# A retention and mixture-of-experts kernel: an attention row's place goes earlier to a weight unit, and work on tables, row ends and decays is moved between queues

## The chip, the core and the metric

The kernel runs on one core of a Trainium2 chip. The metric is the device time of one execution in microseconds (us). Engines are named as in the profile: PE (matrix products), DVE, ACT and POOL (element-wise work), SP (issues DMAs). Each of them takes its instructions in the order in which the program lists them.

## What is computed

Three stages, each feeding the next (reference, cut):

```python
# 1. retention: batch 4, heads 8, sequence 576, head_dim 64
scores = scale * q @ k.T
ret = scores * where(i >= j, gamma[h] ** (i - j), 0)
x = (ret @ v) reshaped to 2304 tokens x 512
# 2. dense layer, d_ff 2048
h = x @ w_in
x = (h * sigmoid(1.702 * h)) @ w_out
# 3. eight experts (d_ff 1024), each token to its best one by cosine similarity
out[mask] = gate_w[mask, None] * (relu(x[mask] @ w1[e]) @ w2[e])
```

## The kernel before, in words

**Attention** (the generator `attention_`) works on 16 "rows" `bp` = batch x pair of heads, 1 MB each from `att` (transposed k and q, then natural k and v), plus the last 64 positions of each sequence ("ends") from `tails` and decay tables `tb` from `tab`. The first 512 positions are four chunks of 128. Rows go in groups, numbered `k` here: group 0 is row 0, group 1 rows 1 and 2, group 2 rows 3 and 4, and so on, group 7 rows 13 and 14, group 8 row 15. For each group PE does: `carried` (state times q, L344), `ends_out` and `scores_end` (L352, L354, L303), `scores` of the next group's first row (L297), `values` (the chunks of this group, L361, between the running states of the next group's rows, L335), then `scores` of the next group's second row. One set of two score banks in PSUM (`sc0`, `sc1`) serves every row, so the next `scores` cannot start before the `masks` of the row before have read them.

- **DVE** does `masks` (L313, two halves), the small products of the ends (L306, L377) and `keep` (L386 or L382: the group's output out of PSUM).
- **ACT** scales each state (L336) and, at the end of a group, splits a row of batches 0 and 1 into a high part (L401) or copies it (L404); for batches 2 and 3 it copies from PSUM (L392).
- **POOL** does `decay` (L319: k times a decay, in place; L323: q too, for batches 2 and 3) two groups ahead of use, and the low parts (L402, `lo = x - hi`). Rows 0 and 2 have their decay on DVE.
- **SP** loads. Nine row places exist; row `bp + 9` takes the place of row `bp` when its group is done. A DMA waits, at its issue, for the landing of the DMA eight places before it.

**The dense layer** needs its 16 weight units. A unit (1 MB, `wd`) is 64-bit floats, taken apart by `convert`, a generator that attention resumes a little at a time (`pull(0.75)`): ACT takes the magnitude (L166) and casts the high half (L169); DVE does five passes over 128x1024 (L179, L181, L189, L194, and L173 for the low half). Units 0 to 2 are loaded into the places of rows 7, 8 and 0 (the latter used a second time by row 9): `WD_AT = (7, 8, 10)` names the rows after whose group the load is issued. Attention resumes `convert` from group 5 on. The dense layer begins with two blocks per unit (L522: layer 1, 12 products of 128x384; L533: layer 2); its first step (`g0`, `g1`, ...: gate by tanh on ACT L553, a product on DVE L555, a cast on ACT L556, a low part on DVE L560) stands in the same DVE and ACT queues as what is left of `convert`. Two banks hold `h`, so the third layer 1 waits until DVE has read the first `h` (L555).

Of the kernel before, what the change touches and what calls it, by code (L numbers as in the profile page):

```python
# [17 lines left out]
P = 128  # L18
# [28 lines left out]
STOP = 1000.0  # L47
WD_AT = (7, 8, 10)
NWD = 3
# [26 lines left out]
def retention_moe_kernel(  # L76
# [77 lines left out]
    def convert():  # L154
# [83 lines left out]
    def attention_(psum):  # L238


        row = [slot(f"row{(i - 2) % NBUF}") for i in range(NBUF)]
        row = row[2:] + row[:2]
        pb, tb = slot("pr"), slot("tb")
# [12 lines left out]
        def load(bp):  # L256
            t = row[bp % NBUF]
            b, pair = divmod(bp, NPAIR)
            if bp and pair == 0:
                SP.dma_start(tl[b], tails[b])  # L260
            if bp == 2:
                SP.dma_start(t[:, AK:], att[bp, :, AK:])
                SP.dma_start(t[:, :AK], att[bp, :, :AK])
            elif bp:
                SP.dma_start(t, att[bp])
            else:
                SP.dma_start(t[:, :AK], att[bp, :, :AK])
                ACT.dma_start(t[:, AK:], att[bp, :, AK:])
                SP.dma_start(tb[:, : TX + TW], tab[:, : TX + TW])
# [23 lines left out]
        def scores(bp):  # L293
            t = row[bp % NBUF]
# [20 lines left out]
        def decay(bp):  # L315
            if bp < NBP:
                kd = row[bp % NBUF][:, AK:AV].rearrange("p (c e) -> p c e", e=HD)
                dec = tbs[:, bp % NPAIR, TK:TS]
                (POOL if bp not in (0, 2) else DVE).tensor_tensor(kd, kd, dec.unsqueeze(2).to_broadcast(kd.shape), ALU.mult)  # L319
                b, pair = divmod(bp, NPAIR)  # L320
                if b > 1:
                    qd = row[bp % NBUF][:, AQ:AK].rearrange("p (c q) -> p c q", q=P)
                    POOL.tensor_tensor(qd, qd, tbs[:, pair, :P].unsqueeze(1).to_broadcast(qd.shape), ALU.mult)  # L323
                    if pair == 0:
                        qe = tl[b][:, :, TQ:TV]
                        POOL.tensor_tensor(qe, qe, tbs[:, :, :TAIL], ALU.mult)

        def state(bp, ch):
            t = row[bp % NBUF]
            if ch == 0:  # L330
# [5 lines left out]
            ACT.activation(kvs[bp % 2][:, 64 * ch : 64 * ch + 64], s, AF.Copy, scale=tbs[:, bp % NPAIR, TS + ch : TS + ch + 1])  # L336

        def carried(bp):
            t, kv = row[bp % NBUF], kvs[bp % 2]
            st["o", bp] = psum.tile([P, 512], F32, tag="o", bufs=2, name=f"ao{bp}")  # L340
            for ch in range(1, NCH):
                for r in heads:
                    o = st["o", bp][r, P * ch : P * (ch + 1)]
                    PE.matmul(o, kv[r, 64 * (ch - 1) : 64 * ch], t[r, AQ + P * ch : AQ + P * (ch + 1)], start=ch == 1, stop=ch == 1, skip_group_check=ch > 1)  # L344

# [10 lines left out]
        def chunk(bp, ch):  # L356
            t, pr = row[bp % NBUF], prs[bp % 3]
            for j, r in enumerate(heads):
                o = st["o", bp][r, P * ch : P * (ch + 1)]
                c0 = AV + P * ch + 64 * j  # L360
                PE.matmul(o, t[:, c0 : c0 + 64], pr[:, 512 * j + P * ch : 512 * j + P * (ch + 1)], start=False, stop=True, skip_group_check=True)  # L361

# [25 lines left out]
        def kept_out(bp):  # L388
# [6 lines left out]
            while c0 < S:  # L395
# [9 lines left out]
                c0 += n  # L405

        def values(rows, nxt):
            out = [(bp, ch) for bp in rows for ch in range(NCH)]
            at = [0, 3, 6, 8] if len(rows) > 1 else [0, 1, 3, 4]

            def states(k):
                for ch in range(NCH):
                    if at[ch] == k:
                        for bp in nxt:
                            state(bp, ch)

            for k, (bp, ch) in enumerate(out):
                states(k)
                chunk(bp, ch)
                if ch == NCH - 1:  # L420
                    keep(bp)
            states(len(out))

# [4 lines left out]
        decay(1)  # L428
        idle(8)
        for ch in range(NCH):  # L430
            state(0, ch)
            idle(3)
        scores_end(groups[0])
        for k, rows in enumerate(groups):
# [8 lines left out]
            for bp in rows:  # L443
                keep_end(bp)
            if k > 5:
                yield False
            if nxt:
                scores(nxt[0])
                if k == 0:
                    decay(2)  # L450
                masks(nxt[0])
            values(rows, nxt)
            for bp in rows:
                if ("o", bp) in st:
                    kept_out(bp)
                if bp in WD_AT:
                    load_wd(WD_AT.index(bp))
                if bp + NBUF < NBP:
                    load(bp + NBUF)
                if bp + NBUF + 1 == NBP:  # L460

# [5 lines left out]
                    load_due()  # L467
            if k > 4:
                yield True
            for bp in nxt[1:]:  # L470
                scores(bp)
                masks(bp)
            if 4 < k < 7:
                yield True
# [474 lines left out]
    for calm in attention():  # L949
        if calm:  # L950
            flush()
        pull(0.75)
    flush()
# [377 lines left out]
```

## Time and profile before

| | us |
|---|---|
| median of 3 runs (722.04 to 722.46) | 722.45 |
| the profiled execution | 720.31 |
| its span | 718.5 |
| PE busy | 700.7 (98%) |
| DVE busy | 452.7 (63%) |
| ACT busy | 307.3 (43%) |
| POOL busy | 205.0 (29%) |

The profiled execution's own time is its span and 1.8 us around it. PE is busy nearly all the time; a product's end is modelled, so a busy PE is not a PE at its peak. Attention takes the first 73 us of the span, the dense layer follows. In the views below, times are from the span's start, "idle before" is how long that engine stood still before the instruction, and behind the arrow stands what ended it.

### The profile page before, as it was taken

Reading aid. Unit: us, or ns where it says so; the run is one execution under the profiler, and the core shown is the slowest. Engines: PE = TensorE matmul, PEld = TensorE weight load, DVE = VectorE, ACT = ScalarE, POOL = GpSimd, SP = SyncE. Lnnn points to the kernel's source line nnn. Section 1 sums busy time; section 2 is a strip of 40 time slices with the busy share of each in tenths; the row PEclk is TensorE's granted clock in tenths of the full one; section 3 lists DMA queues with packets and bytes.
Section 4 is the critical chain, followed back from the end, with each engine's and each line's share of the span. In section 5 each row is a group of like instructions: output and inputs, shape, how many; then the busy total and the mean of one; then the engine's idle time right before and its main releaser. Section 6 shows DMA issues by size and latency. Waiting matters only on the chain. (4 is left out here: it accounts for less than half of the span.)

```text
span 718.5 us, 13118 instructions
## 1 busy us (share of the span) xinstructions
PE 700.7 (98%) x4882; PEld 652.2 (91%) x4882; DVE 452.7 (63%) x1033; ACT 307.3 (43%) x598; POOL 205.0 (29%) x196
## 2 busy tenths in 40 slices
PE   7999899999999999999999999999999999999995
PEld 6898799999999898899998999989999999999994
DVE  3567888888537877765476368656564563564551
ACT  3345445544364333322332243353444545555532
POOL 0791000000000231210110112223446547467553
PEclk9999999999999999999999999999999999999998
DMA  8998999000310031200400311245688879889761
GB/s 336 419 406 281 397 381 307 1 1 1 134 46 1 0 87 47 89 0 1 133 0 1 127 50 58 71 132 143 191 237 252 229 238 271 224 270 259 244 185 63
DMA packets 52724, 113.41 MB, mean 158 GB/s; under 512 B 8098, under 2 KB 28706, under 8 KB 48560
## 3 DMA queue, kind: packets, MB, share of 16 engines
q1 hardware_dynamic: 49312, 102.55, 44.1%
q0 software_dynamic: 3200, 9.46, 3.8%
q8 instruction: 39, 0.64, 0.4%
q10 hardware_dynamic: 144, 0.52, 0.2%
q14 instruction: 29, 0.24, 0.1%
HBM read 84.67 MB, written 28.17 MB: 157 GB/s over the span
## 5 line engine op out<-in xcount | busy, mean ns | idle before, releaser
L522 PE MATMUL h<-x,unit 128*128 128x384 f32 x1152 | 217.8, 337 | 2.3 <-ACT unit L169 1.4
L522 PEld LDWEIGHTS h<-x,unit 128*128 128x128 f32 x1152 | 204.5, 188 | 11.3 <-ACT unit L169 1.7
L220 POOL TENSOR_TENSOR unit<-we,unit 128x512 fp32r<-128x512 f32 x64 | 102.7, 1611 | 117.9 <-ACT unit L218 113.1
L522 PE MATMUL eh<-xt,unit 128*128 128x336 f32 (+6 forms) x672 | 102.1, 301 | 0.0
L522 PEld LDWEIGHTS eh<-xt,unit 128*128 128x128 f32 x672 | 95.5, 188 | 0.4 <-ACT xt L763 0.4
L219 DVE TENSOR_TENSOR unit<-we,unit 128x512 fp32r<-128x512 f32 x64 | 55.7, 870 | 55.8 <-ACT unit L218 55.7
L629 DVE CUSTOM_DVE_ANT_0 dj<-xr,en 128x512 bf16<-128x512 f32 x120 | 78.0, 697 | 0.0
L218 ACT CAST unit<-we 128x1024 fp32r<-128x1024 f32 x64 | 66.8, 1046 | 20.5 <-DMA we<-we 17.6
L595 POOL TENSOR_TENSOR enrm<-scr,c 128x8 f32<-128x8 f32 x1 | 1.7, 1687 | 160.2 <-ACT ej L600 160.2
L572 POOL DMA_INDIRECT out<-y,idx x24 | 24.3, 1011 | 30.3 <-ACT y L795 21.7
L336 ACT ACTIVATE ends<-s,tb 128x64 f32<-128x64 f32 x64 | 17.5, 311 | 35.2 <-PE s L335 35.1
L572 POOL DMA_INDIRECT xs<-xr,slot x18 | 19.4, 1077 | 38.7 <-DVE xr L704 35.3
L689 POOL TENSOR_TENSOR cum<-cum,oh_all 128x8 bf16<-128x8 bf16 x18 | 5.2, 287 | 67.4 <-PE rk L682 52.4
L173 DVE TENSOR_TENSOR unit<-ca,unit 128x1024 fp32r<-128x1024 f32 x16 | 19.5, 1220 | 3.9 <-ACT unit L169 3.9
L297 PE MATMUL sc<-row 64*128 64x128 f32 x256 | 19.0, 285 | 2.4 <-DMA row<-att 1.3
L319 POOL TENSOR_TENSOR row<-row,tb 128x512 f32<-128x512 f32 x14 | 14.6, 1045 | 20.7 <-DMA row<-att 10.8
L495 POOL TENSOR_TENSOR x<-x0s,x 128x768 fp32r<-128x768 f32 x3 | 6.1, 2028 | 48.6 <-ACT x L494 48.6
L189 DVE SCALAR_TENSOR_TENSOR ca<-wd,ca 128x1024 int32<-128x1024 int32 x16 | 19.6, 1223 | 0.4
L795 ACT ACTIVATE y<-y,gate 128x512 f32<-128x512 f32 (+7 forms) x21 | 14.3, 714 | 12.6 <-DMA y<-yd 9.0
L194 DVE SCALAR_TENSOR_TENSOR ca<-wd,ca 128x1024 int32<-128x1024 int32 x16 | 19.5, 1218 | 0.0
L335 PE MATMUL s<-row 128*64 128x64 f32 x256 | 16.3, 234 | 3.1 <-POOL row L319 1.6
L297 PEld LDWEIGHTS sc<-row 64*128 64x128 f32 x256 | 15.8, 187 | 3.8 <-DMA row<-att 1.5
(1311 smaller groups left out, 1523.2 us busy)
## 6 DMA issues: line engine op xcount, KB each, us to landing
we<-we SPq DMA_DIRECT2D x64, 512.0 KB, 4.3
wd<-wd SPq DMA_DIRECT2D x16, 1024.0 KB, 10.6
row<-att SPq DMA_DIRECT2D x14, 1024.0 KB, 14.7
xs<-fill SPq DMA_DIRECT2D x22, 257.0 KB, 10.9
xrow<-xr SPq DMA_DIRECT2D x18, 257.0 KB, 3.7
y<-yd SPq DMA_DIRECT2D x7, 512.0 KB, 4.9
x0d<-x0f SPq DMA_DIRECT2D x4, 768.0 KB, 10.7
x0s<-x0d SPq DMA_DIRECT2D x8, 384.0 KB, 6.7
```

The source lines that it names most:

```text
L173: DVE.tensor_tensor(units[u][:, 1, :], word(u).bitcast(F32), units[u][:, 0, :].bitcast(F32), ALU.subtract)
L189: DVE.scalar_tensor_tensor(a, d[:, :, 1], -0x40000000, a, ALU.bitwise_and, ALU.bitwise_or)
L194: DVE.scalar_tensor_tensor(a, d[:, :, 0], 29, a, ALU.logical_shift_right, ALU.bitwise_or)
L218: ACT.copy(w[:, 0, :], t)
L219: DVE.tensor_tensor(w[:, 1, :512], t[:, :512], w[:, 0, :512].bitcast(F32), ALU.subtract)
L220: POOL.tensor_tensor(w[:, 1, 512:], t[:, 512:], w[:, 0, 512:].bitcast(F32), ALU.subtract)
L297: PE.matmul(scs[j][:, P * ch : P * (ch + 1)], t[r, P * ch : P * (ch + 1)], t[r, AQ + P * ch : AQ + P * (ch + 1)], start=True, stop=True)
L335: PE.matmul(s[r], t[:, AK + c0 : AK + c0 + 64], t[:, AV + c0 : AV + c0 + 64], start=ch == 0, stop=True, skip_group_check=ch > 0)
L336: ACT.activation(kvs[bp % 2][:, 64 * ch : 64 * ch + 64], s, AF.Copy, scale=tbs[:, bp % NPAIR, TS + ch : TS + ch + 1])
L522: PE.matmul(h, w[:, a, P * dc : P * (dc + 1)], xt[:, b, dc, :n], start=k == 0, stop=k == len(terms) - 1)
L572: i = POOL.indirect_dma_start(out=dst[:, :], out_offset=bass.IndirectOffsetOnAxis(ap=rows, axis=0), in_=src, in_offset=None, bounds_check= ...
L629: DVE.tensor_tensor_reduce(junk, r[:, :D], en[e // 4][:, e % 4, :], 1.0, 0.0, ALU.mult, ALU.add, dots[:, E * k + e : E * k + e + 1])
```

## The change

- `EARLY = 5`: places are handed out so that row 5's place is the one that unit 0 will take; unit 0 is loaded when group 3 (rows 5, 6) is done, ahead of row 14. Row 14 takes row 6's place (same moment), row 15 takes row 7's, after group 4. Units 1 and 2 follow rows 8 and 9.
- `convert` is resumed from group 4 on (before: 5), with `pull(0.9)` in place of `pull(0.75)`. In it, the low half of the units 1 and 2 comes one pass earlier in the list.
- The decay tables come in three pieces, and the ends of batches 0 and 1 in two pieces each: first the first pair's, the rest behind the next row or half row.
- `decay` of the rows 7, 8 and 9 goes from POOL to DVE.
- The low parts (POOL) of batch 1 are made in group 6, those of batch 0 once a group is done.
- Row 0's chunks go between its states in place of some products that fill time (`idle`); row 2's scores go between the states of rows 1 and 2, and `idle` products beside them.

```diff
-WD_AT = (7, 8, 10)
+EARLY = 5
+WD_AT = (EARLY, 8, 9)
...
-            if u == 1:
-                low(0)
+            if 0 < u < 4:
+                low(u - 1)
                 yield 1.22
...
-            if u > 1:
+            if u > 3:
                 low(u - 1)
                 yield 1.22
...
-        row = [slot(f"row{(i - 2) % NBUF}") for i in range(NBUF)]
-        row = row[2:] + row[:2]
+        order = [EARLY, NBUF - 1] + [i for i in range(NBUF - 1) if i != EARLY]
+        place = {i: slot(f"row{i}") for i in order}
+        follows = dict(zip(order[2:], range(NBUF, NBP)))
+        row = [place[i] for i in range(NBUF)] + [place[i] for i in order[2:]]
...
+            if bp == 0:
+                SP.dma_start(t[:, :AK], att[bp, :, :AK])
+                ACT.dma_start(t[:, AK:], att[bp, :, AK:])
+                load_tab(0, 1)
+            if pair == 0:
+                load_tails(0, 1 if b < 2 else NPAIR)
             if bp == 2:
                 SP.dma_start(t[:, AK:], att[bp, :, AK:])
+                load_tails(1, NPAIR)
                 SP.dma_start(t[:, :AK], att[bp, :, :AK])
...
             if bp == 1:
-                SP.dma_start(tl[0], tails[0])
-                SP.dma_start(tb[:, TX + TW : n], tab[:, TX + TW :])
+                load_tab(1, 3)
+            if bp == 2:
+                load_tab(3, 4)
+            if bp == 4:
+                load_tails(1, NPAIR)
...
-                (POOL if bp not in (0, 2) else DVE).tensor_tensor(kd, kd, dec.unsqueeze(2).to_broadcast(kd.shape), ALU.mult)
+                (POOL if bp not in (0, 2, 7, 8, 9) else DVE).tensor_tensor(kd, kd, dec.unsqueeze(2).to_broadcast(kd.shape), ALU.mult)
...
-                    POOL.tensor_tensor(lo, src, hi.bitcast(F32), ALU.subtract)
+                    lows.append((b, lo, src, hi.bitcast(F32)))
...
+        new_out(0)
         for ch in range(NCH):
             state(0, ch)
-            idle(3)
+            if ch:
+                chunk(0, ch - 1)
+            idle(2 if ch else 3)
+        chunk(0, NCH - 1)
...
-            if k > 5:
+            if k > 4:
                 yield False
             if nxt:
                 scores(nxt[0])
-                if k == 0:
-                    decay(2)
+            if k == 0:
+                decay(2)
                 masks(nxt[0])
-            values(rows, nxt)
+                keep(0)
+                for ch in range(NCH):
+                    for bp in nxt:
+                        state(bp, ch)
+                    if ch == 1:
+                        scores(nxt[1])
+                        masks(nxt[1])
+                    else:
+                        idle(4)
...
+            make_lows(0 if k < 6 else 1)
+            for bp in rows:
                 if bp in WD_AT:
                     load_wd(WD_AT.index(bp))
-                if bp + NBUF < NBP:
-                    load(bp + NBUF)
-                if bp + NBUF + 1 == NBP:
+                if bp in follows:
+                    load(follows[bp])
+                if follows.get(bp) == NBP - 1:
...
-            if k > 4:
+            if k > 3:
                 yield True
...
-            if 4 < k < 7:
+            if 3 < k < 7:
                 yield True
...
-        pull(0.75)
+        pull(0.9)
```

Three places show what the change does to the order of instructions. First DVE, from the masks of row 4 to those of row 5 (group 2); `row7`, `row8` are the row places, `x3` and `x4` the kept output. Before:

```order
L313 SCALAR_TENSOR_TENSOR pr_89<-sc0_104,tb_90 128x512
L313 SCALAR_TENSOR_TENSOR pr_89<-sc1_105,tb_90 128x512
L306 SCALAR_TENSOR_TENSOR tb_90<-sct_141,tb_90 128x64 x2
L377 TENSOR_TENSOR x3_429<-at3_414,tb_90 128x64
L377 TENSOR_TENSOR x4_431<-at3_414,tb_90 128x64
L313 SCALAR_TENSOR_TENSOR tb_90<-sc0_104,tb_90 128x512
L313 SCALAR_TENSOR_TENSOR tb_90<-sc1_105,tb_90 128x512
```

The same place now:

```order
L328 SCALAR_TENSOR_TENSOR pr_89<-sc0_105,tb_90 128x512
L328 SCALAR_TENSOR_TENSOR pr_89<-sc1_106,tb_90 128x512
L334 TENSOR_TENSOR row7_88<-row7_88,tb_90 128x512
L334 TENSOR_TENSOR row8_81<-row8_81,tb_90 128x512
L321 SCALAR_TENSOR_TENSOR tb_90<-sct_142,tb_90 128x64 x2
L398 TENSOR_TENSOR x3_441<-at3_426,tb_90 128x64
L398 TENSOR_TENSOR x4_443<-at3_426,tb_90 128x64
L328 SCALAR_TENSOR_TENSOR tb_90<-sc0_105,tb_90 128x512
L328 SCALAR_TENSOR_TENSOR tb_90<-sc1_106,tb_90 128x512
```

The decays of rows 7 and 8 now stand on DVE ahead of group 2's ends and of row 5's masks. Second ACT, where attention first resumes `convert`: `wd0` is weight unit 0, `ca0` the work tile. Before, at the end of group 5:

```order
L336 ACTIVATE ends_91<-s11_773,tb_90 128x64
L336 ACTIVATE ends_91<-s12_777,tb_90 128x64
L392 COPY x0f2_95<-ao10_739 128x512
L166 ACTIVATE ca0_819<-wd0_713 128x1024
L375 COPY x0f3_96<-at11_851 128x64
```

Now, at the end of group 4:

```order
L351 ACTIVATE ends_91<-s9_673,tb_90 128x64
L351 ACTIVATE ends_91<-s10_677,tb_90 128x64
L422 CAST x0_1_98<-x7_660 128x192
L425 COPY x0f3_96<-x7_660 128x384
L413 COPY x0f0_93<-ao8_638 128x512
L167 ACTIVATE ca0_726<-wd0_613 128x1024
L396 COPY x0f1_94<-at9_760 128x64
```

The magnitude of unit 0 comes one group earlier, and behind row 7's cast and copy. Third DVE, at the end of attention and the first steps of the dense layer: `unit1`, `unit2` are converted units (the low half is written), `g0t`, `g0l` the dense layer's first step. Before:

```order
L382 COPY x0f3_96<-ao15_1010 128x512
L189 SCALAR_TENSOR_TENSOR ca1_820<-wd1_716,ca1_820 128x1024
L475 CAST ub_68<-uf_608 128x128
L194 SCALAR_TENSOR_TENSOR ca1_820<-wd1_716,ca1_820 128x1024
L179 TENSOR_SCALAR ca0_819<-ca0_819 128x1024
L555 SCALAR_TENSOR_TENSOR g0t_1056<-g0t_1056,h0_1043 128x384
L181 TENSOR_SCALAR ca0_819<-ca0_819 128x1024
L189 SCALAR_TENSOR_TENSOR ca0_819<-wd2_817,ca0_819 128x1024
L173 TENSOR_TENSOR unit1_1062<-ca1_820,unit1_1062 128x1024
L560 TENSOR_TENSOR g0l_1058<-g0t_1056,g0h_1057 128x384
```

Now:

```order
L180 TENSOR_SCALAR ca0_726<-ca0_726 128x1024
L182 TENSOR_SCALAR ca0_726<-ca0_726 128x1024
L403 COPY x0f3_96<-ao15_1030 128x512
L174 TENSOR_TENSOR unit1_1027<-ca1_727,unit1_1027 128x1024
L515 CAST ub_68<-uf_722 128x128
L190 SCALAR_TENSOR_TENSOR ca0_726<-wd2_834,ca0_726 128x1024
L195 SCALAR_TENSOR_TENSOR ca0_726<-wd2_834,ca0_726 128x1024
L595 SCALAR_TENSOR_TENSOR g0t_1076<-g0t_1076,h0_1063 128x384
L180 TENSOR_SCALAR ca_1082<-ca_1082 128x1024
L182 TENSOR_SCALAR ca_1082<-ca_1082 128x1024
L174 TENSOR_TENSOR unit2_1084<-ca0_726,unit2_1084 128x1024
L600 TENSOR_TENSOR g0l_1078<-g0t_1076,g0h_1077 128x384
```

Unit 1 is done before the first step's product, and four passes of unit 2 stand ahead of `g0t`; three more passes stand between `g0t` and `g0l`.

## Rows read from the trace of the kernel before

**Rows 1.** Windows: busy us (and instructions) of PE, PEld, DVE, ACT, POOL, granted clock, DMA share, GB/s.

```profile
30.00:40.00 10.00, 10.00 (x205) 9.29 (x202) 7.01 (x14) 4.95 (x18) 9.11 (x11) 1.00 1.01 414
70.00:80.00 10.00, 7.96 (x78) 6.77 (x75) 8.79 (x12) 4.72 (x9) 0.00 (x0) 1.00 1.00 408
```

**Rows 2.** Timeline (start, us, engine, line, tiles, count, idle before): POOL and PE at row 4.

```profile
21.35 1.04 POOL L319 TENSOR_TENSOR row<-row,tb 128x512 f32<-128x512 f32 x1 [2.42 <-DMA row<-att]
...
22.45 0.34 PE L335 MATMUL s<-row 128*64 128x64 f32 x4 [1.63 <-POOL row L319]
```

**Rows 3.** Timeline: the decay of row 2 on DVE, that of row 8 on POOL.

```profile
12.67 0.69 DVE L319 TENSOR_TENSOR row<-row,tb 128x512 f32<-128x512 f32 x1 [0.48 <-DMA row<-att]
...
32.27 1.04 POOL L319 TENSOR_TENSOR row<-row,tb 128x512 f32<-128x512 f32 x1 [0.89 <-DMA row<-att]
```

**Rows 4.** Timeline: group 2 on PE and DVE, up to the start of group 3.

```profile
26.48 1.53 PE L344 MATMUL ao<-row,ends 64*64 64x128 f32 x24
...
28.75 0.47 DVE L306 SCALAR_TENSOR_TENSOR tb<-sct,tb 128x64 f32<-128x64 f32 x2 [0.76 <-PE sct L303]
29.14 0.34 DVE L377 TENSOR_TENSOR x<-at,tb 128x64 f32<-128x64 f32 x2
...
29.83 1.41 DVE L313 SCALAR_TENSOR_TENSOR tb<-sc,tb 128x512 f32<-128x512 f32 x2 [0.34 <-PE sc L297]
...
32.79 1.16 PE L297 MATMUL sc<-row 64*128 64x128 f32 x16
...
33.88 1.53 PE L344 MATMUL ao<-row,ends 64*64 64x128 f32 x24
```

**Rows 5.** Timeline: PE at the start of the groups 6 and 7.

```profile
56.09 1.53 PE L344 MATMUL ao<-row,ends 64*64 64x128 f32 x24
...
65.06 1.53 PE L344 MATMUL ao<-row,ends 64*64 64x128 f32 x24
```

**Rows 6.** Timeline: ACT at the end of the groups 4 and 5, DVE behind it.

```profile
47.99 0.34 ACT L401 CAST x<-x 128x192 fp32r<-128x192 f32 x1
48.23 0.51 ACT L404 COPY x0f<-x 128x384 f32<-128x384 f32 x1
...
55.39 0.58 ACT L392 COPY x0f<-ao 128x512 f32<-128x512 f32 x1
...
55.85 1.14 ACT L166 ACTIVATE ca<-wd 128x1024 f32<-128x1024 f32 x1
...
57.03 0.69 DVE L179 TENSOR_SCALAR ca<-ca 128x1024 f32<-128x1024 f32 x1 [2.78 <-ACT ca L166]
```

**Rows 7.** Timeline: the first steps of the dense layer.

```profile
72.03 0.21 ACT L375 COPY x0f<-at 128x64 f32<-128x64 f32 x1 [0.18 <-PE at L354]
72.14 1.17 ACT L166 ACTIVATE ca<-wd 128x1024 f32<-128x1024 f32 x1
72.94 4.44 PE L522 MATMUL h<-x,unit 128*128 128x384 f32 x24
...
73.06 0.69 DVE L382 COPY x0f<-ao 128x512 f32<-128x512 f32 x1 [1.18 <-PE ao L361]
...
76.67 0.55 DVE L555 SCALAR_TENSOR_TENSOR g0t<-g0t,h 128x384 f32<-128x384 f32 x1
...
77.25 0.51 ACT L556 CAST g0h<-g0t 128x384 fp32r<-128x384 f32 x1 [1.43 <-DVE g0t L555]
...
78.76 0.61 PE L522 MATMUL h<-x,unit 128*128 128x384 f32 x2 [1.39 <-ACT unit L169]
```

**Rows 8.** Timeline: how that goes on, on PE.

```profile
80.27 2.03 PE L522 MATMUL h<-x,unit 128*128 128x384 f32 x10 [0.89 <-DVE unit L173]
...
82.37 0.40 PE L533 MATMUL o<-unit,g0l 128*128 128x512 f32 x1
```

**Rows 9.** Groups by line and form, 0 to 110 us: count, busy us, mean ns, idle before.

```profile
L189 DVE SCALAR_TENSOR_TENSOR ca<-wd,ca 128x1024 int32<-128x1024 int32 x7 | 8.5, 1219 | 0.1
...
L181 DVE TENSOR_SCALAR ca<-ca 128x1024 int32<-128x1024 int32 x7 | 4.8, 692 | 0.2
```

More of the change, by code (lines that the diff above doesn't have):

```diff
@@ L256, in load, with load_tab, load_tails @@
         def load(bp):
-            t = row[bp % NBUF]
+            t = row[bp]
             b, pair = divmod(bp, NPAIR)
-            if bp and pair == 0:
-                SP.dma_start(tl[b], tails[b])
+            def load_tab(lo, hi):
+                lo, hi = TX * (lo > 0) + TW * lo, TX + TW * hi
+                SP.dma_start(tb[:, lo:hi], tab[:, lo:hi])
+            def load_tails(lo, hi):
+                SP.dma_start(tl[b][:, lo:hi], tails[b, :, lo:hi])
+            if bp == 0:
[4 more added lines that the diff above has]
+                load_tails(0, 1 if b < 2 else NPAIR)
             if bp == 2:
                 SP.dma_start(t[:, AK:], att[bp, :, AK:])
+                load_tails(1, NPAIR)
                 SP.dma_start(t[:, :AK], att[bp, :, :AK])
@@ L265, in load @@
                 SP.dma_start(t, att[bp])
[L266 to L269, printed above, removed]
             if bp == 1:
-                SP.dma_start(tl[0], tails[0])
-                SP.dma_start(tb[:, TX + TW : n], tab[:, TX + TW :])
+                load_tab(1, 3)
[3 more added lines that the diff above has]
+                load_tails(1, NPAIR)
         load(0)
@@ L293, in scores @@
         def scores(bp):
-            t = row[bp % NBUF]
+            t = row[bp]
             for ch in range(NCH):
@@ L328, in state @@
         def state(bp, ch):
-            t = row[bp % NBUF]
+            t = row[bp]
             if ch == 0:
@@ L336, in state, with new_out @@
             ACT.activation(kvs[bp % 2][:, 64 * ch : 64 * ch + 64], s, AF.Copy, scale=tbs[:, bp % NPAIR, TS + ch : TS + ch + 1])
+        def new_out(bp):
+            if ("o", bp) not in st:
+                st["o", bp] = psum.tile([P, 512], F32, tag="o", bufs=2, name=f"ao{bp}")
         def carried(bp):
-            t, kv = row[bp % NBUF], kvs[bp % 2]
-            st["o", bp] = psum.tile([P, 512], F32, tag="o", bufs=2, name=f"ao{bp}")
+            t, kv = row[bp], kvs[bp % 2]
+            new_out(bp)
             for ch in range(1, NCH):
@@ L343, in carried @@
                     o = st["o", bp][r, P * ch : P * (ch + 1)]
-                    PE.matmul(o, kv[r, 64 * (ch - 1) : 64 * ch], t[r, AQ + P * ch : AQ + P * (ch + 1)], start=ch == 1, stop=ch == 1, skip_group_check=ch > 1)
+                    first = ch == 1 and bp > 0
+                    PE.matmul(o, kv[r, 64 * (ch - 1) : 64 * ch], t[r, AQ + P * ch : AQ + P * (ch + 1)], start=first, stop=True, skip_group_check=not first)
         def ends_out(rows):
@@ L356, in chunk @@
         def chunk(bp, ch):
-            t, pr = row[bp % NBUF], prs[bp % 3]
+            t, pr = row[bp], prs[bp % 3]
             for j, r in enumerate(heads):
@@ L360, in chunk @@
                 c0 = AV + P * ch + 64 * j
-                PE.matmul(o, t[:, c0 : c0 + 64], pr[:, 512 * j + P * ch : 512 * j + P * (ch + 1)], start=False, stop=True, skip_group_check=True)
+                first = bp + ch == 0
+                PE.matmul(o, t[:, c0 : c0 + 64], pr[:, 512 * j + P * ch : 512 * j + P * (ch + 1)], start=first, stop=True, skip_group_check=not first)
         def kept_in(bp):
@@ L405, in kept_out, with make_lows @@
                 c0 += n
+        lows = []
+        def make_lows(b):
+            while lows and lows[0][0] <= b:
+                POOL.tensor_tensor(*lows.pop(0)[1:], ALU.subtract)
         def values(rows, nxt):
             out = [(bp, ch) for bp in rows for ch in range(NCH)]
[L409 to L419, printed above, removed]
+            at = [0, 3, 6, 8]
+            for k, (bp, ch) in enumerate(out + [(None, None)]):
+                if k in at and len(rows) + len(nxt) > 1:
+                    for r in nxt:
+                        state(r, at.index(k))
+                if bp is not None:
+                    chunk(bp, ch)
                 if ch == NCH - 1:
                     keep(bp)
-            states(len(out))
         groups = [[0]] + [[bp, bp + 1] for bp in range(1, NBP - 1, 2)] + [[NBP - 1]]
@@ L448, in attention_ @@
                 scores(nxt[0])
-                if k == 0:
-                    decay(2)
+            if k == 0:
+                decay(2)
                 masks(nxt[0])
-            values(rows, nxt)
+                keep(0)
[7 more added lines that the diff above has]
+                        idle(4)
+            else:
+                if nxt:
+                    masks(nxt[0])
+                values(rows, nxt)
             for bp in rows:
@@ L467, in attention_ @@
                     load_due()
-            if k > 4:
+            if k > 3:
                 yield True
-            for bp in nxt[1:]:
+            for bp in nxt[1:] if k else []:
                 scores(bp)
                 masks(bp)
-            if 4 < k < 7:
+            if 3 < k < 7:
                 yield True
```

4 lines of the change are left out of this document (2 added, 2 removed).

## The prediction

> **What bounds the kernel now.** I read the windows first. PE is busy for 10.00 of 10 us in the middle of attention and for 7.96 of 10 where the dense layer begins [rows 1], so an edit gains only where PE stands still or does filling work, and costs wherever it makes PE stand still. Then I read PE's waits in the timeline of the first 85 us, each with what ended it. There are three of note. PE waits 1.63 us for the decay of row 4, which itself started when row 4 landed [rows 2]. It loses time in group 6: groups take 33.88 - 26.48 = 7.40 us from one `carried` to the next [rows 4], group 6 takes 65.06 - 56.09 = 8.97 [rows 5], so 1.57 us more. There DVE stood 2.78 us for ACT's first magnitude, with the masks queued behind it [rows 6]. Last, at the start of the dense layer, PE waits 1.39 and 0.89 us for the two halves of weight unit 1 [rows 7, 8]. Third I read the loads: the DMA engines are busy at a share of 1.01, at 414 GB/s, in the middle of attention [rows 1], so a row lands when its bytes have come through, and POOL's idle time before a decay tells when that is. POOL waited for row 4 until 21.35 [rows 2] and for row 8 until 32.27 [rows 3].
>
> **The start (small tables, row 0's chunks, row 2's scores).** Behind the new order row 4 comes with 295 KB (128 partitions x 576 floats) less ahead of it: 295 KB / 414 GB/s = 0.7 us, so its decay starts near 20.6 and PE goes on near 21.7 in place of 22.45 [rows 2]. PE had 1.63 us to spare there, which pays for what the moved chunks, the filling products and the later rest of the first ends add before it. Sum at that point: -0.7. The bounds are 0 (PE itself comes later) and -1.6 (the whole wait). It will not last, as follows.
>
> **The decays of rows 7 and 8 on DVE.** This decides my forecast. DVE takes its list in order, and the two decays now stand ahead of the ends of group 2 and of the masks of row 5. The bytes ahead of row 8 are the same as before, only cut otherwise, and the engines are full [rows 1], so row 8 lands near 32.2 as before [rows 3]. Before, this wait cost nothing: POOL stood and nobody needed row 8's decay for some microseconds. Now DVE stands until 32.27, and behind it: decay 0.69 [rows 3], ends 0.47 and 0.34, first half of the masks about 0.70 (half of 1.41) [rows 4]: 34.5. Then the first score bank is free for row 6, and the second 0.7 later, at 35.2. PE reached the scores of row 6 at 32.79 and `carried` at 33.88, 1.09 us for eight products in the two banks in turn [rows 4]. Now one product goes at 34.5, the other seven (7/8 x 1.09 = 0.95) at 35.2, and `carried` starts at 36.2. That is **+2.3 us** against before, whatever was gained at the start, since the landing fixes it. The bounds: +1.5 if row 8 lands 0.8 us earlier (more even loads at the start), +3.0 if the small pieces cost that much. Behind it PE runs at its 7.40 us per group again, so nothing gives it back. PE then stands some 1.7 to 2.5 us at one place; it stood 1.39 and 0.89 us close together in the window of rows 1 at a granted clock of 1.00, so I count no loss of clock.
>
> The decay of row 9, also on DVE, finds its row landed (one row more, 1.05 MB / 414 GB/s = 2.5 us after row 8, while DVE is still busy with masks): 0.69 us on an engine that has room, counted 0. POOL is freed of three decays, but PE waits for POOL at row 4 only, whose decay stays: 0.
>
> Here a rule speaks for the change. The Trainium skill, "GPSIMD Engine Reference", section "Engine selection", sends element-wise work on a tile to VectorE, with GPSIMD about twice as slow on two inputs. The trace agrees in direction: 0.69 against 1.04 us for the same tile [rows 2, 3]. By the rule three decays come out 0.35 us shorter each, 1.05 us in all. By the rows it is worth 0, because the price of the move is DVE's place in its list and not the length of the decay.
>
> **Unit 0 a group earlier.** SP issues its load when group 3 is done, with rows 12 and 13 still coming in; it lands some 2.5 us behind row 13, before ACT wants it at the end of group 4. Row 15's load falls behind it and a group later, and is wanted only in group 7: 0. So DVE's wait for ACT's first magnitude moves from group 6 to group 5, and its 1.57 us are not new. But ACT now has row 7's cast and copy (0.34 + 0.51) ahead of the copy of 0.58 and the magnitude of 1.14 [rows 6], and DVE with the masks of row 10 waits that much longer: **+0.8**. Bounds 0 (DVE reaches that place later) and +1.2.
>
> **The start of the dense layer.** Unit 1 is done when the layer begins, so the waits of 1.39 and 0.89 go: -2.28 [rows 7, 8]. What is late next is `g0t`, the product that frees the first `h` bank. In DVE's list now stand, from the magnitude of unit 2 on: two passes of 0.69, row 15's copy (0.69), a low half, a small cast and two passes of 1.22 [rows 7, 9], together 3 x 0.69 + 3 x 1.22 + 0.2 = 5.9 us. The magnitude started at 72.14 and took 1.17 [rows 7]; from 73.3 on this gives `g0t` at 79.2 to 79.8 in before's times, where it was 76.67 [rows 7]. PE's third step of twelve products starts then, at 0.187 us each (2.03 less its tail for ten [rows 8]), and ends at 82.0. Layer 2 needs `g0l`, and ahead of that DVE has two passes and a low half again, the first behind ACT's cast (0.51) and the magnitude of unit 3 (1.17) [rows 7]: 79.8 + 0.51 + 1.17 + 0.69 + 0.69 + 1.22 + 0.55 = 84.6. The product that reads `g0l` ran at 82.37 [rows 8]. So the wait for the unit is replaced by a larger one for DVE: +2.3 by this sum. I take off 0.2, as ACT's small copy (0.21 [rows 7]) now stands behind the magnitude, and 0.6 for eight neighbours in DVE's list that overlap by 0.08 each (28.75 + 0.47 runs past 29.14 [rows 4]): **+1.5**. Bounds: -0.8 (half of the 2.28 comes back, half of the new wait is covered) and +2.3. After that PE is full again in both, and the passes done early are not needed early.
>
> **The rest.** The late low parts of batch 1 (four) lie on POOL after its last decay, some 15 us before the dense layer's second block wants them: 0. Row 9's place frees unit 2 after group 5, and it lands long before its magnitude: 0.
>
> **Sum**: 2.3 + 0.8 + 1.5 = 4.6 us on the profiled execution of 720.31 (span 718.5 and 1.8 around it), so 724.9; the median of the runs stands 2.1 above that execution, and the same difference on 722.45 gives **727.0**. The bounds together are +0.7 and +6.5.
>
> **Rivals.**
> - *No change* (722.5). DVE's hold costs 2.3, but the dense layer's 2.28 comes back whole because ACT and DVE get through their lists faster than I add up. For it: the unit is really ready. Against it: the three passes between `g0t` and `g0l` are in the list.
> - *Faster* (719.5). DVE does not hold at row 8: it would have to land by about 28.8, when DVE began its ends [rows 4]. Then the 0.7 of row 4 stays, and the 2.28 at the dense layer: -3.0. Against it: row 8 landed at 32.27 with full engines, 3.5 us too late, some 1.4 MB of loads. This is also how the change would come out if its moves do what their places suggest and the loads were not the limit.
> - *Much slower* (730 or more). The three waits add to each other, since conversion passes also stand ahead of masks in the groups 6 and 7: +1.6 more for one such place, by the loss of group 6 [rows 5], beyond my upper bounds.
>
> **How the numbers follow.** A run of this kernel tells 0.2% (1.4 us) from no change. I give my forecast 0.80, no change 0.09, faster 0.07, much slower 0.04. The forecast's own spread is about 723.5 to 729; a tenth of it, where the dense layer gives most back, lies within 0.2%. The range from 722.2 to 729.2 takes in the first rival and leaves out the others and the ends. Faster by over 0.2%: 0.08; within: 0.13; slower: 0.79.
>
> **What the profile after would show.** Right: DVE idle for 2 us or more at the decay of row 8 (L334) until about 32.2, ended by the DMA of a row; PE waiting about 1.7 to 2.5 us for DVE at the scores (L312) near 34.5; `carried` of row 5 near 36.2, of row 9 near 51; one longer group, now group 5, of 9.5 to 10 us; no wait for a unit at the dense layer's third step, but one for DVE there and one of 1 to 2.5 us at layer 2's first products. PE busy about as before (one row's filling products fewer or more), the span 4 to 5 us longer. Wrong: a row 8 that lands before 30, or PE at `carried` of row 5 by 34, or layer 2 of the first step less than 9.5 us after the first dense product.

## The result, and the profile after

The changed kernel takes **728.79 us** (median of 6 runs, 727.77 to 730.49), the kernel before 722.46 (6 runs, 719.82 to 725.16): a ratio of 1.009 with a 95% interval of 1.0064 to 1.0116, or 6.3 us more. The forecast was 727.0 in a range of 722.2 to 729.2. The profiled execution took 729.90 us with a span of 728.1, 9.6 us more than before's; PE is busy for 706.6 us in it (97%), where it was 700.7 (98%).

**Row 4** came earlier, as forecast. POOL and PE in the timeline of the changed kernel:

```profile
20.33 1.04 POOL L334 TENSOR_TENSOR row<-row,tb 128x512 f32<-128x512 f32 x1 [1.62 <-DMA row<-att]
...
25.93 1.53 PE L364 MATMUL ao<-row,ends 64*64 64x128 f32 x24
```

The decay starts at 20.33 where it started at 21.35 [rows 2], and `carried` of row 3 at 25.93 in place of 26.48 [rows 4]. PE has no wait of note at row 4 any more (1.63 us before [rows 2]), so only a part of the 1.02 us reaches it.

**The hold at row 8**, in the timeline of DVE and PE:

```profile
32.12 0.69 DVE L334 TENSOR_TENSOR row<-row,tb 128x512 f32<-128x512 f32 x1 [2.75 <-DMA row<-att]
33.38 1.40 DVE L328 SCALAR_TENSOR_TENSOR tb<-sc,tb 128x512 f32<-128x512 f32 x2
34.18 0.49 PE L312 MATMUL sc<-row 64*128 64x128 f32 x2 [1.85 <-DVE tb L328]
34.84 1.16 PE L312 MATMUL sc<-row 64*128 64x128 f32 x14 [0.17 <-DVE tb L328]
35.92 1.53 PE L364 MATMUL ao<-row,ends 64*64 64x128 f32 x24
43.33 1.53 PE L364 MATMUL ao<-row,ends 64*64 64x128 f32 x24
```

DVE stands 2.75 us until row 8 lands at 32.1 (before, POOL waited for it until 32.27 [rows 3]), the ends and masks follow, PE waits 1.85 + 0.17 us, and `carried` of row 5 starts at 35.92 in place of 33.88 [rows 4]. The next group takes 7.41 us, so nothing is made up.

**Group 5**, in the timelines of DVE, POOL and PE:

```profile
50.74 1.53 PE L364 MATMUL ao<-row,ends 64*64 64x128 f32 x24
51.90 1.09 POOL L338 TENSOR_TENSOR row<-row,tb 128x512 f32<-128x512 f32 x1
52.36 1.17 DVE L180 TENSOR_SCALAR ca<-ca 128x1024 f32<-128x1024 f32 x1 [3.47 <-ACT ca L167]
54.98 0.49 PE L312 MATMUL sc<-row 64*128 64x128 f32 x2 [2.01 <-DVE pr L328]
61.29 1.53 PE L364 MATMUL ao<-row,ends 64*64 64x128 f32 x24
68.70 1.53 PE L364 MATMUL ao<-row,ends 64*64 64x128 f32 x24
```

DVE waits 3.47 us for the first magnitude (2.78 before [rows 6]), and its first pass, beside POOL's decay of q at 51.90, takes 1.17 us in place of 0.69. The group takes 61.29 - 50.74 = 10.55 us. Group 6, the long one before, takes 7.41 now. The longer pass is not in every execution: in two later profiles with the same attention (`a2_after_again` and `g1_stuffed_waits` below) it takes 0.69, and PE waits 1.53 us where it waits 2.01 here. In g1, with the clock at 1.00, the group takes 62.45 - 52.38 = 10.07 us:

```profile
52.38 1.53 PE L364 MATMUL ao<-row,ends 64*64 64x128 f32 x24
56.13 0.48 PE L312 MATMUL sc<-row 64*128 64x128 f32 x2 [1.53 <-DVE pr L328]
62.45 1.53 PE L364 MATMUL ao<-row,ends 64*64 64x128 f32 x24
```

**The start of the dense layer**, PE and DVE, and the windows from there with the granted clock (columns as in [rows 1]):

```profile
76.70 4.44 PE L562 MATMUL h<-x,unit 128*128 128x384 f32 x24
82.18 0.55 DVE L595 SCALAR_TENSOR_TENSOR g0t<-g0t,h 128x384 f32<-128x384 f32 x1
82.79 2.38 PE L562 MATMUL h<-x,unit 128*128 128x384 f32 x12 [1.65 <-DVE g0t L595]
86.81 0.55 DVE L600 TENSOR_TENSOR g0l<-g0t,g0h 128x384 fp32r<-128x384 f32 x1
87.42 0.51 PE L573 MATMUL o<-unit,g0l 128*128 128x512 f32 x1 [2.02 <-DVE g0l L600]
90.23 2.97 PE L562 MATMUL h<-x,unit 128*128 128x384 f32 x12
```

```profile
82.00:88.37 6.37, 3.56 (x17) 3.04 (x18) 4.72 (x8) 3.38 (x6) 0.00 (x0) 1.00 1.00 419
88.37:91.78 3.41, 3.41 (x11) 2.92 (x10) 2.75 (x4) 0.98 (x4) 0.00 (x0) 0.50 1.02 431
```

The waits for unit 1 are gone, and in their place stand 1.65 us for `g0t` and 2.02 for `g0l`, both DVE's. Behind them comes what I had counted at nothing: for 3.41 us PE's granted clock is 0.50, the level of 1.2 GHz, and a twelve-product step takes 2.97 us. The same step in the kernel before, and its seventh, in PE's timeline:

```profile
84.22 2.27 PE L522 MATMUL h<-x,unit 128*128 128x384 f32 x12
...
96.78 2.27 PE L522 MATMUL h<-x,unit 128*128 128x384 f32 x12
```

So the step of twelve, the layer's fourth, starts 6.01 us later than before; it was 3.76 at the first dense product (76.70 against 72.94 [rows 7]).

**The rest of the span.** At the dense layer's seventh step, behind the stretch at 0.50, the changed kernel is 6.72 us late (103.50 against 96.78), and the distance stays within 0.2 us of that up to 642 us. The other 3.0 us of this profile come in the last experts, between 642 and 713 us, and 2.0 of them are two waits of PE that the profile of before does not have. In PE's waits over the whole span (in total, how many, the longest):

```profile
PE eo L583 <- ACT unit L219: 1.1, 1, 1.1
PE eh L562 <- DVE eg54l L607: 0.9, 1, 0.9
```

From the 501st of the products `eh`, the experts' first layer, to the last it is 70.7 us here and 67.7 before. `e2_before_decay_dve` below, the kernel before with one edit in attention, takes 70.4 there, and `e1_decay_pool`, the changed kernel but for that edit, 67.4. So nothing shows this part to be the change's, and no sum here contains it.

### The profile page after: what moved, and what is told of

It is laid out like the page before. It is cut to its first block, busy times and chain, and to the rows that moved or that the text cites. A ratio compares the mean times of both kernels' runs of the same rounds, so it can differ in the third digit from the quotient of the medians.

```text
span 728.1 us, 13134 instructions
## 1 busy us (share of the span) xinstructions
PE 706.6 (97%) x4891; PEld 656.4 (90%) x4891; DVE 453.1 (62%) x1036; ACT 307.0 (42%) x598; POOL 205.9 (28%) x193
## 5 line engine op out<-in xcount | busy, mean ns | idle before, releaser
L312 PE MATMUL sc<-row 64*128 64x128 f32 x256 | 21.1, 295 | 5.1 <-DVE pr L328 2.2
L312 PEld LDWEIGHTS sc<-row 64*128 64x128 f32 x256 | 17.4, 196 | 7.0 <-DVE pr L328 2.5
L190 DVE SCALAR_TENSOR_TENSOR ca<-wd,ca 128x1024 int32<-128x1024 int32 x16 | 20.1, 1259 | 0.3
L180 DVE TENSOR_SCALAR ca<-ca 128x1024 f32<-128x1024 f32 x16 | 11.6, 722 | 13.4 <-ACT ca L167 13.4
L803 ACT CAST xt<-tp 128x336 fp32r<-128x336 f32 (+6 forms) x28 | 11.1, 412 | 19.6 <-DVE tp L801 19.6
```

## The experiments

Each kernel was timed in five rounds against the kernel before on the same chip. Whole times from different chips are compared through their ratios to the kernel before.

### The decays, all and alone

`e1_decay_pool` is the changed kernel with one line as it was:

```diff
-                (POOL if bp not in (0, 2, 7, 8, 9) else DVE).tensor_tensor(...)
+                (POOL if bp not in (0, 2) else DVE).tensor_tensor(...)
```

> The changed kernel with one line undone: the decays of rows 7, 8 and 9 are on POOL again. If DVE's hold at row 8 costs what the trace of the changed kernel shows, PE finds row 5's masks ready, row 5's carried starts near 33.0 (0.7 earlier than before, by row 4's earlier landing) and the time falls by about 2.9 us against the changed kernel, to some 3 to 3.5 us over before, as the waits at the start of the dense layer stay. Rival: the loss sits in the new order of the loads (unit 0 ahead of rows 14 and 15, small pieces), and a decay waits for its row on whatever engine: within 1 us of the changed kernel.

`e2_before_decay_dve` is the kernel before with the opposite edit.

> The kernel before with that one line alone: the decays of rows 7, 8 and 9 on DVE. If the hold alone does it: +2.2 us against before, PE waiting 1.75 us or so for DVE at the scores of row 6 near 34, everything behind it shifted by that, the waits at the dense layer unchanged. Rival (the loads do it): within 0.5 us of before.

Measured: e1 724.75 us (723.24 to 726.23), ratio 1.0028 (1.0015 to 1.0041), so 4.5 us under the changed kernel by the ratios (0.90% less 0.28%), more than the 2.9 expected, and 2.0 over before. The intervals are wide enough for 2.9, and a fall of the clock behind the hold, which two later profiles show (below), would go with it. e2 724.26 (721.73 to 728.05), ratio 1.0024 (1.0005 to 1.0043), 0.4 to 3.1 us over before. PE's timeline of e1, then of e2:

```profile
33.29 1.53 PE L364 MATMUL ao<-row,ends 64*64 64x128 f32 x24
75.03 4.43 PE L562 MATMUL h<-x,unit 128*128 128x384 f32 x24
85.79 0.50 PE L573 MATMUL o<-unit,g0l 128*128 128x512 f32 x1 [2.05 <-DVE g0l L600]
87.73 2.27 PE L562 MATMUL h<-x,unit 128*128 128x384 f32 x12
100.48 2.27 PE L562 MATMUL h<-x,unit 128*128 128x384 f32 x12
```

```profile
34.21 0.49 PE L297 MATMUL sc<-row 64*128 64x128 f32 x2 [1.42 <-DVE tb L313]
35.95 2.43 PE L344 MATMUL ao<-row,ends 64*64 64x128 f32 x24
44.94 1.53 PE L344 MATMUL ao<-row,ends 64*64 64x128 f32 x24
```

Without DVE's decays PE does not wait for row 8 (`carried` at 33.29), and with them alone it does (35.95, +2.07 on 33.88 [rows 4]). The hold is the decays' and nothing else's. e1 also gives the price of the dense start with the clock at 1.00 there: 87.73 - 75.03 = 12.70 us from its first product to the fourth step, against 84.22 - 72.94 = 11.28 before, **+1.42**. In e2 the group from 35.95 takes 8.99 us in place of 7.40, though PE has no wait of note in it; the windows show why:

```profile
36.41:39.82 3.41, 3.41 (x46) 3.29 (x44) 1.83 (x4) 0.47 (x2) 3.41 (x5) 0.50 0.99 395
84.20:87.61 3.41, 3.41 (x12) 3.31 (x12) 2.90 (x5) 1.79 (x3) 0.00 (x0) 0.50 1.02 423
```

A stretch at 0.50 behind the wait costs 8.99 - 7.40 = **1.59 us** in this group. The second stretch lies at the start of the dense layer, behind the two waits for unit 1 of 1.39 and 0.89 us that are as in the kernel before; there the clock had stayed at 1.00. This profiled execution took 728.05 us, the longest of e2's twelve, so its profile shows more than its median cost.

### Which decay, and is it the engine or the place in its list?

`h2_row8_pool` gives row 8 alone back to POOL. `h3_decays_behind_masks` leaves all three on DVE, but lists them at the end of the group:

```diff
-(POOL if bp not in (0, 2, 7, 8, 9) else DVE)      # h2
+(POOL if bp not in (0, 2, 7, 9) else DVE)
...
-                if bp > 2:                        # h3
+                if bp > 2 and bp not in (7, 8, 9):
                     decay(bp)
...
                 values(rows, nxt)
+            for bp in then:
+                if bp in (7, 8, 9):
+                    decay(bp)
```

> The changed kernel with the decay of row 8 alone back on POOL; the decays of rows 7 and 9 stay on DVE. Theory 1 (only the load of row 8 holds DVE up; row 7 lands at 28.7 us, in time, and row 9 costs nothing): the wait of PE near 34 us goes, carried of row 5 starts near 33.3 us, and the median is that of the version with all three on POOL (724.75 us), some 4 us under the changed kernel. Theory 2 (all three decays together are too much for DVE): part of the wait stays, half a microsecond or more, and the median lies between 725.5 and 729.

> The changed kernel with the decays of rows 7, 8 and 9 still on DVE, but listed at the end of the group, behind its masks and its kept output, in place of ahead of its ends. Theory 1 (the price of the move is DVE's place in its list, ahead of the masks, and not the engine): DVE waits for no row while masks are due, PE does not wait near 34 us, carried of row 5 starts near 33.3 us, and the median is that of the version with all three on POOL (724.75 us). Theory 2 (DVE has no room for them in these groups, wherever they stand): PE waits 0.7 to 2 us at the next scores or states, and the median stays 726 or more.

Measured: h2 724.78 us (ratio 1.0028, 1.0015 to 1.0042), the same as e1; `carried` of row 5 at 33.37. So row 8 alone made the hold, and rows 7 and 9 on DVE are worth nothing that these runs can tell. h3 728.08 (ratio 1.0069, 1.0052 to 1.0086): a miss of theory 1 in time, though not in its first step. DVE, POOL and PE in h3:

```profile
32.51 2.78 DVE L334 TENSOR_TENSOR row<-row,tb 128x512 f32<-128x512 f32 x2
...
32.38 1.27 POOL L338 TENSOR_TENSOR row<-row,tb 128x512 f32<-128x512 f32 x1 [1.88 <-DMA row<-att]
33.61 1.13 POOL L341 TENSOR_TENSOR more<-more,tb 128x256 f32<-128x256 f32 x1
...
33.33 1.53 PE L364 MATMUL ao<-row,ends 64*64 64x128 f32 x24
36.01 0.49 PE L312 MATMUL sc<-row 64*128 64x128 f32 x2 [0.45 <-DVE pr L328]
41.91 1.53 PE L364 MATMUL ao<-row,ends 64*64 64x128 f32 x24
```

The hold at row 8 is gone (`carried` at 33.33). But the two decays, 0.69 us each in the changed kernel, take 1.69 and 1.17 here (2.78 together), beside POOL's decay of q; POOL's product of 128x256 takes 1.13 (0.68 in the changed kernel). PE waits 0.45 + 0.17 us for the masks behind them, and `carried` of row 7 stands 1.0 us behind e1's (41.91 against 40.95). The Trainium skill, "SBUF — State Buffer", section "Who interferes with whom", says that a VectorE instruction with two inputs in SBUF contends with a GpSimd instruction that reads SBUF. The trace agrees: a decay has both inputs in SBUF, and 0.69 became 1.69 and 1.17. It is not DVE that is late each time. In the changed kernel POOL worked beside the decay of row 8 as well, and there the decay, begun at 32.12, kept its 0.69, while POOL's decay of q, begun 0.05 us later, took longer (1.28 in the kernel before):

```profile
32.17 1.78 POOL L338 TENSOR_TENSOR row<-row,tb 128x512 f32<-128x512 f32 x1 [1.39 <-DMA row<-att]
```

So both theories hold a part: the place in the list made the 2 us, and where DVE has time for the decays POOL runs too, and they were twice as long. Group 5 was longer too (PE waits 2.25 us there, 1.52 in e1), and the profiled execution has two stretches at 0.50, one more than e1's.

### What is listed between attention and the dense layer

`e3_no_last_pull` is the changed kernel without the last piece of conversion, `e4_both` is e3 with e1's line:

```diff
     flush()
-    pull(2.4)
+    pull(0.0)
```

> The changed kernel without the passes of convert that are taken between attention and the dense layer (pull(2.4) becomes pull(0.0)). If the two passes of 1.22 us that stand ahead of the first step's product on DVE make PE's waits there (1.65 and 2.02 us in the changed kernel), both go, DVE comes 2.44 us earlier, and PE reaches the fourth layer 1 some 4 us earlier than in the changed kernel. If the low clock behind these waits (0.50 from 88.4 us for 3.4 us) comes of PE standing still, it goes too and brings another 1.7: 4 to 5.5 us under the changed kernel, 0.5 to 2 over before. Rival: the units that were put off are missed at the next steps, and the waits come back there: within 1 us of the changed kernel. Rival on the clock: it falls at this place in any case, 1.00 is not held.

> The decays on POOL again and no passes between attention and the dense layer. If the two losses are independent, their gains add: 7 to 8.5 us under the changed kernel, 1 to 2 us under before. Rival: one gain covers the other (PE only comes earlier to the next wait): no better than the better of the two alone.

Measured: e3 726.28 us (723.26 to 729.76), ratio 1.0047 (1.0028 to 1.0067): by the ratios 3.1 under the changed kernel (0.9% less 0.47%), less than the 4 to 5.5 expected, and widely spread; its profiled execution, at 723.74, has no stretch at 0.50 between 15 and 700 us. e4 **721.23** (719.68 to 722.73), ratio 0.9977 (0.9965 to 0.9989): 1.7 us faster than before, as expected, and 3.5 under e1. PE in e4:

```profile
51.87 0.48 PE L312 MATMUL sc<-row 64*128 64x128 f32 x2 [1.51 <-DVE pr L328]
74.81 6.53 PE L562 MATMUL h<-x,unit 128*128 128x384 f32 x36
83.31 2.27 PE L562 MATMUL h<-x,unit 128*128 128x384 f32 x12
86.45 0.50 PE L573 MATMUL o<-unit,g1l 128*128 128x512 f32 x1 [0.63 <-DVE g1l L600]
96.96 2.27 PE L562 MATMUL h<-x,unit 128*128 128x384 f32 x12
```

The first 36 products run through, and from the first to the fourth step it is 8.50 us, 4.20 less than in e1. A part of it is lost again, as the rival of e3 said: up to the seventh step it is 96.96 - 74.81 = 22.15 us, where e1 takes 100.48 - 75.03 = 25.45 and the kernel before 23.84 (96.78 - 72.94). So the passes are worth 3.30 us here, and the dense layer's start is 1.6 us slower than before with them and 1.7 faster without them. A unit that is ready is worth something only once the passes ahead of `g0t` and `g0l` are out of DVE's list.

### Where the conversion is resumed

`e5_old_resumption` is e1 with the conversion resumed as in the kernel before; `g2_no_waits_but_start` is e4 with a pause behind the first magnitude, so that DVE's first pass is listed behind the next masks:

```diff
-            if k > 4:                             # e5
+            if k > 5:
                 yield False
...
-            if k > 3:
+            if k > 4:
                 yield True
...
-            if 3 < k < 7:
+            if 4 < k < 7:
...
-        pull(0.9)
+        pull(0.75)
...
         magnitude(0)                              # g2
+        yield 0.9
         for u in range(NF1):
```

> The changed kernel with the decays of rows 7, 8 and 9 on POOL and the conversion resumed as before (from group 5 on, the smaller amount, the last piece ahead of the dense layer kept). Theory 1 (resuming a group earlier moves the list of DVE so that the dense layer waits for g0t and g0l): the long group is the sixth again, of about 9 us, the waits of 1.66 and 2.05 us turn back into waits for the halves of unit 1 of about 1.4 and 0.9, and with the 0.7 us that row 4 gains the median is 0.3 to 1 us under before, so 2 us under the version with POOL's decays alone (724.75). Theory 2 (the resumption is not what costs): the time stays near 724.7.

> The version that had decays of rows 7, 8 and 9 on POOL and nothing resumed between attention and the dense layer (721.23 us), with one more edit: the first resumption of the conversion issues ACT's first magnitude alone, and DVE's first pass comes one resumption later, behind the masks of the second row of the pair. Theory 1 (the masks behind DVE's wait for that magnitude are what makes group 5 long): the wait of 1.51 us before the scores there goes, group 5 takes about 7.4 us, and the median falls by 1.7 us to some 719.5. Theory 2 (the conversion is only pushed back, and PE waits for it at the start of the dense layer instead): waits of 1 to 2 us there, median near 721.

Measured: e5 723.13 us (720.58 to 725.01), ratio 1.0012 (0.9994 to 1.0029). By the ratios that is 1.2 us under e1, in the direction of theory 1, but the two intervals overlap, and it is not under before: the dense start is as it was (waits of 1.37 and 0.64, 11.00 us to the fourth step), and row 4's gain was lost again (`carried` of row 13 at 65.01, 65.06 before [rows 5]). I had not expected that; the passes there (0.89 and 0.96 us in place of 0.69) run beside POOL's late low parts, which fits h3 but was not tried by itself.

g2 takes **719.10 us** (717.96 to 720.51), ratio 0.9956 (0.9940 to 0.9972), 3.2 us under before, by the ratios 1.5 under e4 (1.7 expected), and the best version of the study. PE in g2:

```profile
48.44 1.53 PE L365 MATMUL ao<-row,ends 64*64 64x128 f32 x24
50.60 1.16 PE L313 MATMUL sc<-row 64*128 64x128 f32 x16
55.93 1.53 PE L365 MATMUL ao<-row,ends 64*64 64x128 f32 x24
87.83 0.50 PE L574 MATMUL o<-unit,g2l 128*128 128x512 f32 x1 [0.60 <-DVE g2l L601]
```

PE does not wait at the scores, group 5 takes 55.93 - 48.44 = 7.49 us, and the masks behind DVE's wait were indeed what made it long. Of theory 2 there is a rest: some waits of 0.2 to 0.8 us in the dense layer, and 23.54 us from its first step to the seventh, 1.4 more than in e4.

### The clock

`a2_after_again` is the changed kernel as it is. `g1_stuffed_waits` puts small products in front of the two waits of the dense layer, into a bank that layer 2 starts anew (`i == 2` is the third layer 1, `blk == 0` the first layer 2):

```diff
+    def stuff(n):
...
+        for _ in range(n):
+            PE.matmul(o[:64, :P], ones[:, :64], ones, start=True, stop=True)
...
+        if i == 2:
+            stuff(14)
...
+            if blk == 0:
+                stuff(18)
```

> The changed kernel as it is, on the same chip as the three runs beside it. Theory 1 (the two waits at the start of the dense layer, 1.65 and 2.02 us, cost their length in every execution, and a granted clock of 0.50 behind them is added only in some): the median lies near 728, executions spread over 2 to 3 us, and the profiled one shows the same two waits, with or without a stretch at 0.50 behind them. Theory 2 (the clock falls there in every execution of this kernel): the profiled execution shows a stretch of about 3.4 us at 0.50 near 88 us again.

> The changed kernel, with 14 and 18 small products (about 0.093 us each, so 1.3 and 1.7 us) in front of PE's two waits at the start of the dense layer, into a bank that the next layer overwrites; DVE's and ACT's lists are as they were. Theory 1 (the part of the loss that my sum lacked is the clock behind these waits): the rests of the waits are near 0.3 us each, the third and the fourth step of the layer start when they did (82.8 and 90.2 less nothing), the granted clock stays at 1.00 between 80 and 95 us, and the median is up to 1.7 us (3.41 us at half speed) under that of the changed kernel beside it. Theory 2 (the waits alone make the loss, and the fall of the clock seen there was chance): same median within 0.5 us.

Measured: a2 730.62 us (728.79 to 731.70), ratio 1.011 (1.0091 to 1.0128); g1 729.90 (727.95 to 732.80), ratio 1.0111 (1.0087 to 1.0134). Windows of a2 at its three falls of the clock, and of g1 at its only one and at the dense start:

```profile
34.13:40.96 6.83, 6.83 (x66) 6.32 (x66) 4.63 (x7) 1.43 (x4) 5.41 (x6) 0.50 1.02 414
58.03:61.44 3.41, 3.41 (x34) 3.19 (x36) 3.41 (x5) 0.53 (x2) 3.41 (x3) 0.50 0.06 19
92.16:95.57 3.41, 3.41 (x11) 3.12 (x10) 2.40 (x4) 0.99 (x3) 0.00 (x0) 0.50 1.01 423
```

```profile
36.15:39.57 3.42, 3.42 (x47) 3.42 (x44) 1.97 (x3) 0.72 (x3) 3.42 (x4) 0.50 1.01 414
80.00:92.00 12.00, 10.56 (x76) 9.15 (x75) 10.29 (x14) 4.26 (x7) 0.00 (x0) 1.00 1.02 427
```

a2 fell behind each of its three places of waiting, at 34, 57 and 91 us; the profiled execution of the changed kernel above fell at the last alone. In g1 the stuffing shortened the waits to 0.72 and 0.71 us and the clock stayed at 1.00 there, but it fell behind the hold at row 8. The ratios of a2 and g1 are the same, so no gain of stuffing the dense waits shows, as theory 2 has it; but their intervals reach 1.3 and 1.7 us to each side, so a gain of the 1.7 us of theory 1 is not excluded. Whether stuffing prevents falls there can't be told from one profile either, as e1 with the same waits unstuffed did not fall there. Of a2's own theories, its profile shows the fall at the dense start again; e1 and h2 have the same two waits without one, which speaks against a fall in every execution. Its median, 730.62, is above the 728 of theory 1.

## Why the prediction was right, and where its sum was off

The forecast (slower, 727.0) held, and by the mechanism that it named: the terms that it adds up sum to 4.6 to 5.1 us in the traces, where it said 4.6. The median moved by 6.3, and what lies between has no term in the forecast. Term by term, as read in the traces:

| term | predicted | measured | from |
|---|---|---|---|
| row 4, swallowed later | -0.7 | -0.55 | 25.93 against 26.48 |
| DVE's hold at row 8 | +2.3 | +2.04 | 35.92 against 33.88 |
| unit 0 a group earlier | +0.8 | +1.1 to +1.6 | group 5 of 10.07 (g1) and 10.55, against group 6 of 8.97 before |
| dense layer's start, clock at 1.00 | +1.5 | +1.42 | e1, from first product to fourth step |
| loss of clock | 0 | +1.0 to +1.6 for each stretch of 3.41 us | h2's group 5, 11.05 against g1's 10.07; e2's group of 8.99 |

- **The decays on DVE** (+2.3): right in place, cause and size. Row 8 landed at 32.12 (forecast 32.2), PE went on at 34.18 (34.5). e1, e2 and h2 show cause and size: row 8 alone, through DVE's list. Rows 7 and 9 and POOL's relief are 0, as counted, as far as h2 and e1 can tell. The 1.05 us that the Trainium skill's rule ("GPSIMD Engine Reference", section "Engine selection") gave did not come.
- **Unit 0 a group earlier** (+0.8, bounds 0 and 1.2): too small, at 1.1 in g1 still inside its bounds and at 1.6 in the profile above beyond them. ACT did come later, by nearly what "DVE with the masks of row 10 waits that much longer" says: DVE's wait is 3.47 against 2.78. What the step lacked is the passes behind it. In the profile above the first one was longer too, 1.17 against 0.69, beside POOL's decay, and those 0.48 us are the difference of PE's waits, 2.01 and 1.53; a later pass (L190) takes 1.80 in a2 and g1 as well, 1.22 before. I took durations from rows where POOL stood still. g2 shows that the wait could be avoided altogether.
- **The start of the dense layer** (+1.5): right at a clock of 1.00, with the two waits where the list of DVE put them. e4 shows that the passes in that list are the cause. Up to the seventh step it is +1.6.
- **"So I count no loss of clock"**: wrong. My evidence was one window of before with waits of 1.39 and 0.89 us and a clock of 1.00, and that was chance: behind the same two waits the clock fell in e2. Behind the new waits of 1.5 to 2.3 us it fell in some executions and not in others. The sum of the other terms is 2.04 + 1.42 and 1.1 to 1.6, so 4.6 to 5.1 us; the median moved by 6.3, and in a2, timed again beside before, by 1.1%, or 7.9. The mean granted clock of all runs goes the same way: 0.9933 for the changed kernel, 0.9905 in a2, where the kernel before had 0.9955 and g2 0.9965 on the same chip. A thousandth of clock is at most 0.73 us of 728, so in a2 up to 3.6 us went with the clock. That is an estimate, an upper bound.
- **The profile**: the span grew by 9.6 us and not by 4 to 5, and PE was busy 5.9 us longer and not as before. The 6.7 us up to the dense layer's seventh step are the terms above and one stretch at 0.50; the other 3.0 came in the last experts, where the forecast had nothing. That the median lies only 1.8 us from 727.0 is in part luck: none of these losses was in the forecast, and the same kernel timed again (a2, 730.62) is outside its range.
- The rival *no change* fell because `g0t` and `g0l` did wait, the rival *faster* because row 8 landed at 32.1. Of *much slower* a part came true, by another way than its own: the waits did not add to each other in the groups 6 and 7, but the clock added to them.

What is open: which waits the clock falls behind, and so how the 6.3 us of the median divide between waits, clock and the last experts in a given execution; what makes PE wait in the last experts; and why e5 lost row 4's gain again.

## What to carry to other kernels

Before an operation that waits for a load is moved to another engine, look up what is queued behind it there: on POOL the same wait for row 8 cost nothing, on DVE it held the masks and so PE for 2 us, with a shorter instruction. Weights made ready earlier pay only when the conversion for the next ones does not stand ahead of the operations that the matrix engine waits for next; here the same early unit is a loss of 1.6 us or a gain of 1.7 up to the dense layer's seventh step, by what is listed at one place. And a wait of PE costs more than its length where the clock can fall behind it, so its price has a spread, and the whole time gets one too (e2 721.7 to 728.1, g2 718.0 to 720.5). The clock is not all of that spread, as the last experts took up to 3 us more in one profile than in another.

## What was not expected of the hardware

- **The clock falls behind waits of 1.4 to 2.3 us, but not behind each.** In the eleven traces of the changed kernels twelve stretches at 0.50 lie between 15 and 700 us (a2's of 6.83 us counted once; the last 4 to 7 us of the span, at 0.50 in every trace, before's too, are left out), all of them at the three places of this study: scores of row 6, scores of group 5, dense start. Each begins within 2 us of the end of a wait of PE there. e3 waited 2.02 and 1.75 us and e5 1.38 and 1.37 without a fall, and the profiles of the kernel before and of g2 have none.
- **DVE and POOL slow each other on operands in SBUF**, now the one, now the other: decays of 0.69 us took 1.69 and 1.17 beside POOL (h3), a pass over 128x1024 1.17 in place of 0.69, and POOL's product of 0.68 took 1.13; beside other work of POOL the decays kept their 0.69. In the first 130 us of the twelve traces every decay and every pass over 128x1024 on DVE that overlaps no work of POOL takes its usual time (0.68 to 0.70, or 1.21 to 1.23), and all that take longer overlap it. Durations that a trace shows for one engine are those beside the neighbours that it had there.
